# A linear attention block on one core: two row tiles transposed by DMA instead of TensorE, the fold's matmuls reordered, and the last row tile cut in four

## The chip, the cores and the metric

The kernel runs on one core of a Trainium2 chip. A core has a matrix engine (TensorE, PE in the profile, with PEld for its weight loads), a vector engine (DVE), a scalar engine (ACT), GpSimd (POOL) and a sync engine (SP), each with its own instruction queue, and sixteen DMA engines that SP's and ACT's queues feed here. Matmuls write to PSUM, eight banks of 512 float32 columns in 128 partitions; everything else lives in SBUF. The metric is the device time of one execution in microseconds (us), as the median of the runs.

## The reference

One batch of S = 2048 rows, D = 640 columns, 32 heads of 20 columns, all bfloat16.

```python
qkv = (x @ wqkv) split into q, k, v, each [32 heads, S, 20]
phi = lambda t: jnp.where(t > 0, t + 1, jnp.exp(t)) + 1e-6
pq, pk = phi(q), phi(k)
kv = jnp.einsum("bhsd,bhse->bhde", pk, v)
z = jnp.einsum("bhsd->bhd", pk)
num = jnp.einsum("bhqd,bhde->bhqe", pq, kv)
den = jnp.einsum("bhqd,bhd->bhq", pq, z)[..., None] + 1e-6
return (num / den, heads joined to [S, 640]) @ wo
```

## The kernel before, in words

The whole program is straight-line. A small planner (`Plan`) takes operations in the order in which the Python code adds them, puts each on the list of its engine, and works out from named reads and writes which semaphores it has to wait for. So each engine's order is the order of the calls, and where two calls are swapped, the work of every engine that they use is swapped. PSUM banks are named by hand.

**Load and k (0.8 to 27.8 us).** For k = x @ wk the matmul needs x with its columns on the partitions (`xT`). Row tiles have 128 rows. The first four, rows 0 to 511, are loaded as they are (`load_xn`, from SP's and ACT's queues, L230) and turned by TensorE against an identity (`transpose_x`, L194; DVE copies the result out of PSUM, L199). The constant NPE = 4 sets how many. All later rows come by the DMA's crossbar transpose, issued on SP's queue (`load_xT`, L184): first one load of 128 rows, then five of 256 and one of 128. The first of them waits until the last slice of wk has landed (L186). Behind them on SP's queue stand the loads of `load_rest`: wq, the plain x of row tiles 4 to 15 in three pieces, wv, wo. The k matmuls (`k_half`, L278) of row tiles 0 and 1 go column block by column block, in the order in which the slices of wk land, with the transposes of tiles 2 and 3 between; from tile 2 on a tile is ten matmuls of 320 columns, into two of eight banks, and ACT and DVE make phi of it (`k_phi`, L291 to L296).

**State by way of p (27.8 to 60.6 us).** Instead of v the kernel accumulates p = x^T phi(k) over all sixteen row tiles, one half of the columns at a time, five accumulators in banks 0 to 4 (`p_step`, L305), then copies the accumulators out, three by ACT and two by DVE (`p_out`, L317 and L320). DVE adds up z beside it. Between these matmuls stand single q tiles (`next_q` calls `q_tile`): five matmuls of 512 columns (L331), an exp on ACT (L339), two passes on DVE (L341, L344). There are twenty q tiles, four blocks of 512 rows by five column blocks; they use banks 5, 6 and 7 in turn (`take`).

**The fold (60.6 to 75.3 us).** When p is complete, the kernel (a) computes the eleventh q tile; (b) the normaliser of the first 1024 rows (`inverse`: sum matmuls L454, on ACT the logarithm L464 and exp L466, which gives a reciprocal) and spreads it over the partitions by DMA on SP's queue (`den_spread`, L471); (c) the state kv = wv^T p in 30 short matmuls (`kv_group`, L408) and cuts it to the heads' diagonal blocks on DVE (`kv_mask`, L425); (d) multiplies the state by wo in six pairs of matmuls (`w2_group`, L432), which ACT copies out (L436) and SP's queue lays out anew in `w2p` (`w2_rows`, L443). A q tile stands before each pair but the fifth, four more follow. In these q tiles' wake the five normalising multiplies of the first 512 rows run on DVE (`scale` fills a list, and each `next_q` takes one from it; `normalize`, L479).

**Output (75.3 us to the end).** A row tile of the output is pq @ w2p, two halves of five matmuls of 320 columns (`out_tile`, L487), copied out half by ACT (L509) and half by DVE (L512) and stored by SP's queue (L497). The normaliser of the second 1024 rows follows the second tile. The first tile needs the first 512 rows normalised and all of w2p. The last row tile (`out_last`) is cut in pieces of 320 and 160 columns (ACT) and 160 (DVE); SP stores the first 480 columns, ACT's queue the other 160.

Of the kernel before, what the change touches and what calls it, by code (L numbers as in the profile page):

```python
# [82 lines left out]
def bass_standalone__linear_attn_block__prompt_kernel(nc, x, wqkv, wo, out):  # L83
    B, S, D = x.shape
    assert (B, S, D) == (1, 2048, 640)
    H, DH = 32, 20
    NC_ = D // 128
# [7 lines left out]
    with contextlib.ExitStack() as ctx:  # L95
# [49 lines left out]
        def pool_const():  # L145
# [28 lines left out]

        NPE = 4
        XCH = [(128 * t, 128 * t + 128) for t in range(NPE + 1)] + [
            (a, min(a + 256, S)) for a in range(128 * NPE + 128, S, 256)]

# [3 lines left out]
        def load_xT():  # L182
            for i, (a, b) in enumerate(XCH[NPE:]):
                P.add("sp", lambda e, a=a, b=b: e.dma_start_transpose(  # L184
                    xT[:, :].rearrange("p (c s) -> p c s", s=S)[:, :, a:b], x[0, a:b, :]),
                    reads=[("wk", 4)] if i == 0 else [],  # L186
                    writes=[("xT", NPE + i)], dma=True)

# [36 lines left out]
        def load_wk():  # L225
            tl = mybir.InstLoadActFuncSet(
                name=nc.get_next_instruction_name(),
                act_func_set_id=ACT_TABLE_SET_LN_EXP, ins=[], outs=[])
            P.add("act", lambda e: e.add_instruction(tl), writes=["table"])
            for eng, what in (("sp", "x01 w01 w23 w45 x34"), ("act", "x12 w12 w34 x23")):  # L230
                for k in what.split():
                    a, b = int(k[1]), int(k[2])
                    if k[0] == "x":
                        load_xn(a, b, eng)
                    else:
                        P.add(eng, lambda e, a=a, b=b: e.dma_start(
                            wk[:, a * D:b * D].rearrange("p (c n) -> p c n", n=D),
                            wqkv[128 * a:128 * b, D:2 * D].rearrange("(c p) n -> p c n", p=128)),
                            writes=[("wk", c) for c in range(a, b)], dma=True)
# [4 lines left out]
        def load_rest():  # L244
            w_cols(wqn, 0, D, 0, "wqn", "sp")
            for a, b in ((4, 8), (8, 12), (12, 16)):
                load_xn(a, b, "sp")
# [76 lines left out]

        def q_tile(sbk, c, b):
            i = nq[0] % 3
            nq[0] += 1

            def mm(e):
                for d in range(NC_):  # L330
# [8 lines left out]
            P.add("act", lambda e: e.activation(t[:, :], bank(b), ACTF.Exp),  # L339
                  reads=[("bank", b), "table"], writes=[("eq", i)])  # L340
            P.add("dve", lambda e: e.tensor_scalar(  # L341
                t[:, :], t[:, :], 1.0, 1e-6, ALU.min, ALU.add),
# [85 lines left out]

        def w2_group(g, b):
            n = gsz[g]  # L430
            for h in range(2):
# [3 lines left out]
                    reads=[("kvt", g), "wog", "wog5"], writes=[("bank", b + h)])  # L435
            P.add("act", lambda e: e.copy(  # L436
                fold(w2g[0:n, g * D:(g + 1) * D]), two_banks(b, parts=n)),
                reads=[("bank", b), ("bank", b + 1)], writes=[("w2g", g)])

        def w2_rows(g):  # L440
# [54 lines left out]
        def out_dma(st, lo, hi, eng="sp"):  # L495
            j = st % 4
            P.add(eng, lambda e: e.dma_start(  # L497
                out[0, 128 * st:128 * st + 128, lo:hi], osb[j][:, lo:hi]),
                reads=[("osb", j, c) for c in range(lo // 160, hi // 160)],
                writes=[("out", st, lo)], dma=True)  # L500
            out_keys.append(("out", st, lo))
# [3 lines left out]
        def out_evac(st, b, lo, hi, eng):  # L505
            j = st % 4
            keys = [("osb", j, c) for c in range(lo // 160, hi // 160)]
            if eng == "act":
# [13 lines left out]
        def out_last(st, b):  # L522
            q = HALF // 2
            for n, (lo, hi, eng) in enumerate(((0, HALF, "act"), (HALF, HALF + q, "act"),
                                               (HALF + q, D, "dve"))):
                out_mm(st, b[n], lo, hi)
                out_evac(st, b[n], lo, hi, eng)
            out_dma(st, 0, HALF + q)
            out_dma(st, HALF + q, D, "act")

# [5 lines left out]
        warm(512, 512, 512, 512, 512, 512)  # L536
        order = "t0 t1 k00 k01 k10 k11 k02 k12 k03 k13 t2 k04 k14 t3"
        for k in order.split():
# [22 lines left out]

        def next_q(n=1):
            q_tile(*qs.pop(0), take())
            for _ in range(n):
# [24 lines left out]
        next_q()  # L589
        for st in range(NT):  # L590
            p_step(1, st)
# [37 lines left out]
        for st in range(4, NT - 1):  # L629
# [3 lines left out]
            out_tile(st, 2 * (st % 4) if st > 5 else 2 * (st % 2))  # L633
        out_last(NT - 1, (6, 7, 0))

# [36 lines left out]
```

## Time and profile before

| | us |
|---|---|
| median of 3 runs (101.2 to 102.3) | 101.67 |
| the profiled execution | 101.73 |
| its span, from first to last instruction | 100.0 |
| TensorE busy in it | 96.8 |
| DVE busy | 69.2 |
| ACT busy | 43.3 |

The profile is one execution on the hardware. Its page gives busy times by engine, a line of 40 equal slices of the span per engine (tenths of each slice), the chain of work that ended last, and groups of like instructions with their count, total and mean (ns) and, behind the bar, the idle time ahead of them. A timeline gives start, length, engine, line, operation, tiles and count; neighbours of one kind are merged, and PEld rows are left out where they only repeat PE. "SPq" and "ACTq" are queues that issue DMAs: their length is the issue, not the transfer; the time from issue to landing is a view of its own. Matmuls are pipelined: the time of one (0.3 us for 320 columns) is longer than the distance between two. Some matmul records can be missing, so that a count may be one short.

### The profile page before, as it was taken

The numbers are of one execution on the slowest core, as the hardware profiler recorded it, in microseconds if no ns is written. First come the engines' busy times: TensorE is split into PE (matmuls) and PEld (weight loads), VectorE is DVE, ScalarE is ACT, GpSimd is POOL, SyncE is SP. The second block draws the span as 40 slices with busy tenths as digits, with TensorE's granted clock in tenths as the row PEclk, the third lists the DMA queues.
The fourth block names the chain that finished last, engine by engine and source line by source line (L and its number), as shares of the span: only waits on it lengthen the run. The fifth ranks groups of instructions, "written<-read, shape, count | busy, mean of one in ns | idle before, by whom it ended". The sixth has DMA issues, their size and how long they took to land.

```text
span 100.0 us, 1793 instructions
## 1 busy us (share of the span) xinstructions
PE 96.8 (97%) x697; PEld 63.0 (63%) x703; DVE 69.2 (69%) x140; ACT 43.3 (43%) x76; POOL 3.3 (3%) x15
## 2 busy tenths in 40 slices
PE   6999999999999999999999999999999999999992
PEld 2556777777777565656667565756446677777771
DVE  0217988888889379799996445758899759853331
ACT  5005554445697220462132227398954523333322
POOL 6600000000000000000000000000000000000000
PEclk9999999999999999999999999999999999999999
DMA  2963999699999900000000000014440324523333
GB/s 56 308 226 71 185 205 137 132 236 377 371 365 289 191 14 0 0 3 0 7 0 0 0 0 0 25 34 123 120 136 1 117 70 153 213 95 120 131 131 131
DMA packets 17076, 11.93 MB, mean 119 GB/s; under 512 B 8749, under 2 KB 17069, under 8 KB 17069
## 3 DMA queue, kind: packets, MB, share of 16 engines
q1 hardware_dynamic: 16349, 11.14, 42.9%
q10 hardware_dynamic: 720, 0.70, 2.1%
q8 instruction: 5, 0.08, 0.3%
q14 instruction: 2, 0.02, 0.1%
HBM read 5.90 MB, written 2.62 MB: 85 GB/s over the span
## 4 chain that ended last, share of the span: by engine, by line
PE 91%; DVE 4%; ACT 2%; issue 1%
PE ps L278 22%; PE ps L487 22%; PE ps L305 22%; PE ps L331 16%; PE ps L269 3%; DVE pq L344 2%; PE ps L194 2%; PE ps L408 2%; PE ps L454 1%; ACT eq L339 1%; DVE pq L479 1%; PE ps L432 1%; DVE eq L341 1%; ACT w2g L436 1%; DVE osb L512 0%
## 5 line engine op out<-in xcount | busy, mean ns | idle before, releaser
L305 PE MATMUL ps<-pk,xn 128*128 128x320 bf16 x160 | 23.5, 299 | 0.0
L331 PE MATMUL ps<-xT,wqp 128*128 128x512 bf16 x94 | 23.1, 379 | 0.3
L278 PE MATMUL ps<-wk,xT 128*128 128x320 bf16 x160 | 22.8, 302 | 0.0
L487 PE MATMUL ps<-w2p,pq 128*128 128x320 bf16 (+1 forms) x165 | 22.1, 295 | 0.1
L339 ACT ACTIVATE eq<-ps 128x512 bf16<-128x512 f32 x20 | 12.0, 599 | 21.2 <-PE ps L331 20.7
L305 PEld LDWEIGHTS ps<-pk,xn 128*128 128x128 bf16 x160 | 15.6, 98 | 7.4 <-DVE pt L320 0.2
L487 PEld LDWEIGHTS ps<-w2p,pq 128*128 128x128 bf16 x165 | 15.8, 98 | 6.6 <-DVE pq L479 0.6
L278 PEld LDWEIGHTS ps<-wk,xT 128*128 128x128 bf16 x160 | 15.4, 99 | 6.6 <-DMA wk<-in_wqkv_dram 0.4
L291 ACT ACTIVATE ek<-ps 128x640 bf16<-128x640 f32 x16 | 11.2, 704 | 14.7 <-PE ps L278 14.7
L331 PEld LDWEIGHTS ps<-xT,wqp 128*128 128x128 bf16 x100 | 9.7, 97 | 9.0
L344 DVE SCALAR_TENSOR_TENSOR pq<-ps,eq 128x512 bf16<-128x512 f32 x20 | 13.8, 692 | 0.7
L296 DVE SCALAR_TENSOR_TENSOR pk<-ps,ek 128x640 bf16<-128x640 f32 x16 | 13.2, 825 | 0.5
L512 DVE CAST osb<-ps 128x320 bf16<-128x320 f32 (+1 forms) x16 | 7.7, 479 | 8.3 <-PE ps L487 8.2
L509 ACT CAST osb<-ps 128x320 bf16<-128x320 f32 (+1 forms) x17 | 7.0, 417 | 13.4 <-PE ps L487 12.1
L341 DVE TENSOR_SCALAR eq<-eq 128x512 bf16<-128x512 bf16 x20 | 5.8, 292 | 9.8 <-ACT eq L339 9.7
L479 DVE TENSOR_TENSOR pq<-pq,rd 128x512 bf16<-128x512 bf16 x20 | 7.7, 416 | 0.4 <-DMA rd<-rdc 0.4
L293 DVE TENSOR_SCALAR ek<-ek 128x640 bf16<-128x640 bf16 x16 | 5.2, 325 | 2.0 <-ACT ek L291 1.9
L199 DVE COPY xT<-ps 128x256 bf16<-128x256 bf16 (+1 forms) x8 | 2.2, 318 | 6.1 <-PE ps L194 6.1
L350 DVE TENSOR_TENSOR za<-pk 128x1280 f32<-128x1280 bf16 x4 | 5.8, 1481 | 0.0
L350 DVE TENSOR_TENSOR za<-za 128x1280 f32<-128x1280 f32 x3 | 4.4, 1480 | 0.0
L259 ACT COPY wqp<-wqn 128x640 bf16<-128x640 bf16 x5 | 4.3, 939 | 0.0
L436 ACT CAST w2g<-ps 120x640 bf16<-120x640 f32 (+1 forms) x6 | 4.0, 690 | 0.0
(38 smaller groups left out, 33.2 us busy)
## 6 DMA issues: line engine op xcount, KB each, us to landing
out_dram<-osb SPq DMA_DIRECT2D x15, 160.0 KB, 1.8
xn<-in_x_dram SPq DMA_DIRECT2D x3, 640.0 KB, 8.0
wqn<-in_wqkv_dram SPq DMA_DIRECT2D x1, 800.0 KB, 5.6
wv<-in_wqkv_dram SPq DMA_DIRECT2D x1, 800.0 KB, 11.2
wog<-in_wo_dram SPq DMA_DIRECT2D x1, 750.0 KB, 13.5
w2p<-w2g SPq DMA_DIRECT2D x5, 150.0 KB
rd<-rdc SPq DMA_DIRECT2D x8, 64.0 KB, 2.3
wk<-in_wqkv_dram SPq DMA_DIRECT2D x3, 160.0 KB, 4.4
```

Of the source, the lines that this page charges most:

```text
L278: r = e.matmul(bank(b + h, HALF), xT[:, c * S + 128 * st:c * S + 128 * st + 128], wk[:, c * D + HALF * h:c * D + HALF * (h + 1)], start=(c ...
L291: P.add("act", lambda e: e.activation(fold(t[:, :]), two_banks(b), ACTF.Exp), reads=banks + ["table"], writes=[("ek", st % 3)])
L296: P.add("dve", lambda e: e.scalar_tensor_tensor(fold(pk[:, st * D:(st + 1) * D]), two_banks(b), 0.0, fold(t[:, :]), ALU.max, ALU.add), rea ...
L305: r = e.matmul(bank(d, HALF), xn[:, st * D + 128 * d:st * D + 128 * d + 128], pk[:, st * D + HALF * h:st * D + HALF * (h + 1)], start=(st ...
L331: r = e.matmul(bank(b), wqp[:, d * D + 128 * c:d * D + 128 * c + 128], xT[:, d * S + BK * sbk:d * S + BK * (sbk + 1)], start=(d == 0), sto ...
L339: P.add("act", lambda e: e.activation(t[:, :], bank(b), ACTF.Exp), reads=[("bank", b), "table"], writes=[("eq", i)])
L344: P.add("dve", lambda e: e.scalar_tensor_tensor(pq[:, c * S + BK * sbk:c * S + BK * (sbk + 1)], bank(b), 0.0, t[:, :], ALU.max, ALU.add), ...
L350: P.add("dve", lambda e: e.tensor_tensor(d_ap, a, b, ALU.add), reads=ra + rb, writes=[dst])
L479: P.add("dve", lambda e: e.tensor_tensor(v, v, rd[i][:, BK * o:BK * (o + 1)], ALU.mult), reads=[("rd", i, 2 * o), ("rd", i, 2 * o + 1), (" ...
L487: r = e.matmul(bank(b, hi - lo), pq[:, c * S + 128 * st:c * S + 128 * st + 128], w2p[:, c * D + lo:c * D + hi], start=(c == 0), stop=(c == ...
L509: P.add("act", lambda e: e.copy(osb[j][:, lo:hi], bank(b, hi - lo)), reads=[("bank", b)], writes=keys)
L512: P.add("dve", lambda e: e.tensor_copy(osb[j][:, lo:hi], bank(b, hi - lo)), reads=[("bank", b)], writes=keys)
```

## The change

Three edits.

Crossbar: NPE goes from 4 to 2. Row tiles 2 and 3 get their transposed rows by two crossbar loads of 128 rows, ahead of six of 256; the first waits for the first slice of wk instead of the last. Their two transposes on TensorE go, and so do the early plain loads of x for tiles 2 and 3 on ACT's and SP's queues. That x is still needed for p: `load_rest` now loads tiles 2 to 15 in pieces of four, five and five.

Fold: the last two row tiles of p are accumulated in turn, bank by bank. The state matmuls and masks are added inside the eleventh q tile, between its exp and its DVE passes, and so stand ahead of the normaliser. DVE instead of ACT copies out the first pair, which stands right behind the normaliser's sum. Banks 4, 6, 7, 5 serve the q tiles after that. The multiplies of the first 512 rows are taken two behind the thirteenth q tile and one behind each of the next three; pairs three and four stand side by side; five q tiles follow the last pair instead of four. (`w2_rows` is called by `w2_group` itself.)

Last row tile: four pieces of 320 (ACT), 160 (DVE), 96 (ACT) and 64 columns (DVE) in four banks. The stores stay at 480 columns by SP and 160 by ACT's queue. The keys by which the planner follows the output are 32 columns wide instead of 160.

```diff
-        NPE = 4
-        XCH = [(128 * t, 128 * t + 128) for t in range(NPE + 1)] + [
-            (a, min(a + 256, S)) for a in range(128 * NPE + 128, S, 256)]
+        NPE = 2
+        XCH = [(128 * t, 128 * t + 128) for t in range(NPE + 2)] + [
+            (a, min(a + 256, S)) for a in range(128 * NPE + 256, S, 256)]
...
-                    reads=[("wk", 4)] if i == 0 else [],
+                    reads=[("wk", 0)] if i == 0 else [],
...
-            for eng, what in (("sp", "x01 w01 w23 w45 x34"), ("act", "x12 w12 w34 x23")):
+            for eng, what in (("sp", "x01 w01 w23 w45"), ("act", "x12 w12 w34")):
...
-            for a, b in ((4, 8), (8, 12), (12, 16)):
+            for a, b in ((2, 6), (6, 11), (11, 16)):
...
-        def q_tile(sbk, c, b):
+        def q_tile(sbk, c, b, between=None):
...
+            if between:
+                between()
             P.add("dve", lambda e: e.tensor_scalar(
...
-        def w2_group(g, b):
+        def w2_group(g, b, eng="act"):
...
-            P.add("act", lambda e: e.copy(
+            P.add(eng, lambda e: (e.copy if eng == "act" else e.tensor_copy)(
                 fold(w2g[0:n, g * D:(g + 1) * D]), two_banks(b, parts=n)),
                 reads=[("bank", b), ("bank", b + 1)], writes=[("w2g", g)])
+            w2_rows(g)
...
         def out_last(st, b):
-            q = HALF // 2
-            for n, (lo, hi, eng) in enumerate(((0, HALF, "act"), (HALF, HALF + q, "act"),
-                                               (HALF + q, D, "dve"))):
+            for n, (lo, hi, eng) in enumerate(((0, HALF, "act"), (HALF, 480, "dve"),
+                                               (480, 576, "act"), (576, D, "dve"))):
                 out_mm(st, b[n], lo, hi)
                 out_evac(st, b[n], lo, hi, eng)
-            out_dma(st, 0, HALF + q)
-            out_dma(st, HALF + q, D, "act")
+            out_dma(st, 0, 480)
+            out_dma(st, 480, D, "act")
...
-        order = "t0 t1 k00 k01 k10 k11 k02 k12 k03 k13 t2 k04 k14 t3"
+        order = "t0 t1 k00 k01 k10 k11 k02 k12 k03 k13 k04 k14"
...
-        for st in range(NT):
+        for st in range(NT - 2):
             p_step(1, st)
...
+        for d in range(NC_):
+            p_step(1, NT - 2, (d,))
+            p_step(1, NT - 1, (d,))
         p_out(1)
-        next_q()
+
+        def state_groups():
+            kv_group(0)
+            kv_mask(0)
+        next_q(between=state_groups)
         inverse(0)
         den_spread(0, (0, 1))
-        kv_group(0)
-        kv_mask(0)
-        small[:] = [5, 6, 7, 4]
-        for g in range(NG):
-            if g != 4:
-                next_q()
-            w2_group(g, 2 * ((g + 1) % 2))
-            w2_rows(g)
-            if g == 1:
-                scale(0, 0)
+        small.insert(0, 4)
+        w2_group(0, 2, "dve")
+        next_q()
+        w2_group(1, 0)
+        scale(0, 0)
+        next_q(2)
+        w2_group(2, 2)
+        w2_group(3, 0)
+        next_q()
+        w2_group(4, 2)
+        next_q()
+        w2_group(5, 0)
         den_spread(0, (2, 3))
-        for _ in range(4):
+        for _ in range(5):
             next_q()
...
-        out_last(NT - 1, (6, 7, 0))
+        out_last(NT - 1, (6, 7, 0, 1))
```

More of the change, by code (lines that the diff above doesn't have):

```diff
@@ L498, in out_dma @@
                 out[0, 128 * st:128 * st + 128, lo:hi], osb[j][:, lo:hi]),
-                reads=[("osb", j, c) for c in range(lo // 160, hi // 160)],
+                reads=[("osb", j, c) for c in range(lo // 32, hi // 32)],
                 writes=[("out", st, lo)], dma=True)
@@ L506, in out_evac @@
             j = st % 4
-            keys = [("osb", j, c) for c in range(lo // 160, hi // 160)]
+            keys = [("osb", j, c) for c in range(lo // 32, hi // 32)]
             if eng == "act":
@@ L560, in take, with next_q @@
             return small[-1]
-        def next_q(n=1):
-            q_tile(*qs.pop(0), take())
+        def next_q(n=1, between=None):
+            q_tile(*qs.pop(0), take(), between)
             for _ in range(n):
```

## The prediction

> **What bounds the kernel now.** I read the page first: the busy shares, the slices, the chain that ended last.
>
> ```profile
> span 100.0 us, 1793 instructions
> PE 96.8 (97%) x697; PEld 63.0 (63%) x703; DVE 69.2 (69%) x140; ACT 43.3 (43%) x76; POOL 3.3 (3%) x15
> PEclk9999999999999999999999999999999999999999
> GB/s 56 308 226 71 185 205 137 132 236 377 371 365 289 191 14 0 0 3 0 7 0 0 0 0 0 25 34 123 120 136 1 117 70 153 213 95 120 131 131 131
> PE 91%; DVE 4%; ACT 2%; issue 1%
> ...
> L331 PE MATMUL ps<-xT,wqp 128*128 128x512 bf16 x94 | 23.1, 379 | 0.3
> L278 PE MATMUL ps<-wk,xT 128*128 128x320 bf16 x160 | 22.8, 302 | 0.0
> ...
> rd<-rdc SPq DMA_DIRECT2D x8, 64.0 KB, 2.3
> ```
>
> TensorE is busy 97% of the span and carries 91% of the chain, at full granted clock in every slice. So an edit saves only what it takes off TensorE's list, what it closes of TensorE's few gaps, and what follows the last matmul. A busy share can hide matmuls that wait, so next I looked stage by stage, by windows (length; busy time of PE, PEld, DVE, ACT, POOL; clock; DMA).
>
> ```profile
> 27.80:60.60 32.80, 32.64 (x218) 20.79 (x220) 24.97 (x40) 11.88 (x20) 0.00 (x0) 1.00 0.24 63
> 60.60:75.30 14.70, 14.48 (x109) 8.06 (x110) 11.25 (x27) 10.74 (x21) 0.00 (x0) 1.00 0.27 75
> ```
>
> From 27.8 to 60.6 us no more than 0.16 us is open, and the change touches nothing there that TensorE waits for. In the fold (60.6 to 75.3) 0.22 us is open. That leaves three places: the first 12 us, the end of the fold, and the tail.
>
> **Part 1: rows 256 to 511 by the crossbar.** The timeline of the start (start, length, what):
>
> ```profile
> 4.72 2.73 PE L278 MATMUL ps<-wk,xT 128*128 128x320 bf16 x16
> ...
> 7.38 0.45 PE L194 MATMUL ps<-ident,xn 128*128 128x128 bf16 x5
> ...
> 7.67 0.71 PE L278 MATMUL ps<-wk,xT 128*128 128x320 bf16 x4
> ...
> 8.21 0.44 PE L194 MATMUL ps<-ident,xn 128*128 128x128 bf16 x5
> ...
> 8.49 7.78 PE L278 MATMUL ps<-wk,xT 128*128 128x320 bf16 x55
> ```
>
> A matmul of 320 columns is on record for 0.302 us (L278 above), so the last of a row starts 0.30 before the row's end, and the last row gives (7.78 - 0.30)/55 = 0.136 us a matmul and 1.36 us a row tile (ten of them). Before, row tile 2 starts at 8.49 and tile 4 at 8.49 + 2 x 1.36 = 11.21. The two L194 rows go away. The sixteen matmuls of the first row leave TensorE free at 4.72 + 2.73 - 0.30 + 0.14 = 7.29, four more follow (0.54), and tile 2 could start at 7.83: **0.66 us saved**. Four copies of DVE (L199) go too; they stood beside TensorE's matmuls, so they count nothing.
>
> Now tiles 2, 3 and then 4 must come by crossbar in time. The queue's waits, the issues on SP's queue, and the times from issue to landing:
>
> ```profile
> SPq L184 <- DMA wk<-in_wqkv_dram: 4.0, 1, 4.0
> ```
>
> ```profile
> 1.26 0.42 SPq L236 DMA_DIRECT2D wk<-in_wqkv_dram  x1
> ...
> 7.13 1.33 SPq L184 DMA_TRANSPOSE xT<-in_x_dram  x1
> ...
> 8.51 1.37 SPq L184 DMA_TRANSPOSE xT<-in_x_dram  x1
> ...
> 17.12 2.00 SPq L184 DMA_TRANSPOSE xT<-in_x_dram  x1
> ```
>
> ```profile
> wk<-in_wqkv_dram SPq DMA_DIRECT2D x1, 160.0 KB, 3.2
> ...
> xT<-in_x_dram SPq DMA_TRANSPOSE x1, 3.0
> ...
> xT<-in_x_dram SPq DMA_TRANSPOSE x1, 4.1
> ...
> xT<-in_x_dram SPq DMA_TRANSPOSE x1, 4.0
> ...
> DMA to landing us min/median/max: 3.0/4.4/6.1
> ```
>
> The four rows of landings belong to the four issues above them, in order; the last row is over all seven crossbar loads. Before, the first load (128 rows) waits for the last weights and goes out at 7.13; it lands at 10.1. The second (256 rows) goes out at 8.51 and lands at 12.6, the seventh lands at 21.1. The change lets the first go when the first weights land, 1.26 + 3.2 = 4.5. Call its loads X1 and X2 (128 rows each), then X3 to X8 (256 each). Issues follow each other at 1.38 us (7.13 to 8.51), whatever their rows:
> - X1 goes at 4.5, lands at 7.5, and tile 2 is due at 7.83: no wait.
> - X2 goes at 5.9, lands at 8.9, and tile 3 is due at 9.19: no wait.
> - X3 goes at 7.25. It is the first load of 256 rows behind one of 128, as the 8.51 row is, so 4.1 us: it lands at 11.35. Tile 4 is due at 7.83 + 2 x 1.36 = 10.55. **TensorE waits 0.80 us**, and tile 4 starts at 11.35 instead of 11.21.
>
> So the matmuls leave and a new wait takes their time: net +0.14. This wait has no row in the trace of before, so it has bounds. Below: with the shortest landing of any load, 3.0, X3 lands at 10.25 and there is no wait (0). Above: at the median, 4.4, the wait is 1.1; at the longest, 6.1, it is 2.8. I take 4.1, by the row of the same size and place. If X1 or X2 is late by some tenths, that costs nothing more, since X3 is what ends last.
>
> The loads behind X3: from 12.6 (row 896) to 21.1 (row 2048) the stream brought 256 rows in 1.9 us, and TensorE uses them in 2.72. No further wait. On SP's queue one plain load of x goes away ahead of the crossbar loads and one crossbar load is added; ACT's queue loses one load. At 1.9 us for 256 rows X8 lands at 11.35 + 5 x 1.9 = 20.9 against 21.1, so the loads queued behind it (wq, the rest of x in three uneven pieces, wv, wo) keep their times.
>
> Here the Trainium skill speaks against my wait. Its page "Advanced Engine Details and Errata", section "X-Bar Transpose (TRN2)", says that "TRN2 transpose DMAs are as fast as regular DMAs". The trace of before does not agree: the GB/s row has 205, 137 and 132 in the slices from 12.5 to 20.0 us, where crossbar loads run, and 377, 371 and 365 from 22.5 to 30.0, where plain loads do. By that rule X3 (0.33 MB) would need 0.9 us behind X2, an estimate at the plain loads' 371 GB/s, and TensorE would not wait: the sum would be -1.01 instead of -0.21.
>
> **Part 2: the fold.** Its timeline:
>
> ```profile
> 60.63 1.08 ACT L317 CAST pt<-ps 128x320 bf16<-128x320 f32 x3 [1.44 <-PE ps L305]
> ...
> 61.60 0.73 PE L454 MATMUL ps<-pq,zb 128*32 128x256 bf16 x20
> ...
> 62.27 1.61 PE L408 MATMUL ps<-pt,wv 128*128 128x120 bf16 x30
> ...
> 62.89 0.42 ACT L466 ACTIVATE rdc<-lb 128x256 bf16<-128x256 f32 x1
> 63.34 1.32 SPq L471 DMA_DIRECT2D rd<-rdc  x2
> 63.53 0.94 DVE L425 TENSOR_TENSOR kvt<-ps,bm 120x480 bf16<-120x480 f32 x3 [0.17 <-PE ps L408]
> ...
> 70.76 4.48 PE L331 MATMUL ps<-xT,wqp 128*128 128x512 bf16 x19
> ...
> 73.61 0.41 DVE L479 TENSOR_TENSOR pq<-pq,rd 128x512 bf16<-128x512 bf16 x1
> ...
> 74.87 0.41 DVE L479 TENSOR_TENSOR pq<-pq,rd 128x512 bf16<-128x512 bf16 x1
> ...
> 75.34 2.89 PE L487 MATMUL ps<-w2p,pq 128*128 128x320 bf16 x20
> ```
>
> TensorE's gap is at its end. The last q matmul starts at 70.76 + 4.48 - 0.38 = 74.86 (0.38 by L331's mean) and the next could start 0.22 later (nineteen starts in 4.10 us), at 75.08; the output matmuls start at 75.34, when the fifth normalising multiply (74.87 + 0.41) is done. **0.26 us** is lost. After the change the five multiplies stand behind q tiles 13 (two), 14, 15 and 16, and the last no longer behind tile 18. DVE's spacing there is 1.26 us a tile (73.61 to 74.87), so two tiles earlier is 2.5 us earlier: the wait goes.
>
> What comes late instead: the normaliser. The state matmuls (1.5 us) go ahead of its sum, so its reciprocal ends 1.5 later, at 64.8, and the first two spreads go out at 64.85 and 65.5. The page's median for such a spread is 2.3 us; with 3.0 they land by 68.5. Tile 13 leaves TensorE about 66.3 (63.6, then two pairs of 0.27 and two tiles of 1.08), so the first multiplies may wait up to 2 us on DVE, and the copies and q passes behind them with it. The fifth follows three tiles (3 x 1.26) after: 72.7 at the latest, against the 75.08 at which the output wants it.
>
> TensorE's own list in the fold is the same (ten q tiles, sum, state, six pairs). New waits on it: the state matmuls now start one q tile after the last accumulation (61.5) and need all five copies of the accumulated banks. In the order of before the last copy ends at 60.63 + 1.08 = 61.71; pairing the last two row tiles bank by bank frees the first bank 8 matmuls (1.1 us) before the last, so copies end near 61.1: no wait, and without that cover 0.2. The first pair of state-times-wo needs the masks: these start 1.26 behind the state matmuls (62.27 to 63.53) and take 0.94, so 62.8 to 63.7, while the pair is due behind state (1.45) and sum (0.66, from 61.60 to 62.27), at 63.6: 0 to 0.1. DVE takes one copy of 640 columns from ACT: between one and two of its copies of 320 columns (0.49, in the tail below), so up to 1.0 us, and it had 14.70 - 11.25 = 3.4 us free. Pairs 2 and 3 now stand side by side and need the banks of pairs 0 and 1 copied out; ACT had 4.0 us free, so I put that wait between 0 and 0.3, and take 0. With bank 4, long free, first in line, no q tile waits for a bank. I take -0.26, with 0 as the other end, since every margin is a few tenths and the gap to win is no larger.
>
> **Part 3: the last row tile.** The tail:
>
> ```profile
> 96.69 0.49 DVE L512 CAST osb<-ps 128x320 bf16<-128x320 f32 x1 [0.87 <-PE ps L487]
> 97.37 0.64 ACT L509 CAST osb<-ps 128x320 bf16<-128x320 f32 x2 [0.93 <-PE ps L487]
> 98.06 0.32 DVE L512 CAST osb<-ps 128x160 bf16<-128x160 f32 x1 [0.88 <-PE ps L487]
> 98.42 0.35 ACTq L497 DMA_DIRECT2D out_dram<-osb  x1
> ```
>
> ```profile
> 53.95 0.39 PE L390 MATMUL ps<-ones,zh 128*128 128x1 bf16 x10
> ```
>
> Matmul columns stay 640, in four pieces instead of three: five more matmuls, but of the same total length if short ones keep their pace. The last copy shrinks from 160 to 64 columns. Between 320 columns (0.49) and 160 (0.32) a column costs 1.06 ns of DVE, so 0.10 off; the ten short matmuls cost about 0.01 more. ACT's copy of 96 columns ends ahead of it, and the last transfer keeps its 40 KB. **-0.09**; at worst 0.
>
> The price of short matmuls is bounded by the last row: ten matmuls of one column, each with its own weights, lie within 0.39 us, so less than 0.043 apart. At the pace of 320 columns in 0.136, 96 columns take 0.041 and 64 take 0.027: held up by 5 x 0.016 = 0.08 at most, and I take 0. The Trainium skill, page "TensorE: Matmul & The Clock Gate", section "Wait — 56ns, not 53.3ns?", gives two floors, about 25 ns and, with hardware decode off, about 62 ns a matmul. By the second the pieces of 96 and 64 columns would cost 0.62 instead of 0.34 us, 0.28 more, an estimate from that page; the bound of 0.043 in this trace excludes it, so the sum goes without.
>
> **The sum.** The profiled execution took 101.73: a span of 100.0 and 1.73 around it; the median of the three runs is 101.67, so they are one case. -0.66 + 0.80 - 0.26 - 0.09 = **-0.21**, so 101.5.
>
> **Rivals.**
> - *Crossbar loads keep up* (14%). X3 lands by 10.8, next to nothing waits. For it: the first load took 3.0, not 4.1. Against: 10.1 to 12.6 is 2.5 us for the next 256 rows. -0.66 - 0.26 - 0.09 = -1.01: 100.7. It is also where the Trainium skill's rule above would lead.
> - *Weights hold the stream back: slower* (11%). Issued at 4.5, X1 stands in SP's queue behind weights that land until 7.1. If it moves only then, it lands 3.0 - 1.3 later at 8.8, X2 1.25 after, X3 2.5 after that, at 12.55: tile 4 is 1.34 late against 11.21, -0.35 for the rest, so 102.7. For it: 226 GB/s still moving in the slice from 5.0 to 7.5. Against: two loads of x are gone from these queues, and X1 needs only to land by about 7.8, not to be first. It decides from about 12.5 on.
> - *The fold gains nothing* (5%): a late spread or mask takes the 0.26 back: 101.8.
> - My forecast holds the other 70%, X3 between 10.8 and 12.3.
>
> **Chances.** About 1% is what a measurement can tell from no change, 1.02 us here. Faster takes half of the first rival and a little of the forecast: 0.11. Slower is the second rival: 0.12. The rest is within 1%: 0.77. Range: from the first rival's 100.7 to just short of the second's, 102.5.
>
> **What would show it.** Right: the first crossbar issue at 4.5; TensorE idle just under 1 us ahead of tile 4, ended by a crossbar load; output matmuls following the last q tile with no gap; a last copy of 64 columns near 0.22 us. Wrong: a wait ahead of tile 2 (second rival), none at all (first), or a q tile waiting for DVE.

## The result and the profile after

The changed kernel takes 101.56 us (median of 22 runs, 101.09 to 101.97) against 101.68 us for the kernel before (22 runs). The ratio is 0.9996, with a 95% interval of 0.9977 to 1.0016: no change that can be told, where 101.5 and "within 1%" were forecast. The profiled execution took 101.59 us. Its page:

```profile
span 100.1 us, 1780 instructions
...
PE 96.2 (96%) x692; PEld 62.7 (63%) x698; DVE 68.6 (68%) x138; ACT 43.0 (43%) x75; POOL 3.2 (3%) x15
...
PE 84%; DMA 8%; SPq 3%; DVE 2%; issue 1%; ACT 1%
...
L278 PE MATMUL ps<-wk,xT 128*128 128x320 bf16 x160 | 22.6, 301 | 0.7 <-DMA xT<-in_x_dram 0.7
```

TensorE has 0.6 us less work (96.8 before), but its share of the chain that ended last fell from 91% to 84%: DMA and SP's queue, which that row of the kernel before does not list, now hold 11%. The k matmuls (L278), which had no idle time ahead of them, have some, and a crossbar load ends it. The chain of waits of the changed kernel names the loads (start, length, what):

```profile
1.27 3.22 DMA wk<-in_wqkv_dram
4.51 1.33 SPq L184
5.88 1.26 SPq L184
7.18 4.54 DMA xT<-in_x_dram
...
11.77 16.47 PE ps L278 x120
```

Read it as a sentence: the first weights land at 4.49, SP issues two crossbar loads of 128 rows in a row, then X3, the first of 256 rows; that takes 4.54 us, and only then does TensorE go on, with row tile 4. From there TensorE is nearly all of the chain, as before. The same start in the timeline of TensorE's matmuls:

```profile
4.93 3.08 PE L278 MATMUL ps<-wk,xT 128*128 128x320 bf16 x20
8.45 3.05 PE L278 MATMUL ps<-wk,xT 128*128 128x320 bf16 x20 [0.43 <-DMA xT<-in_x_dram]
11.77 2.89 PE L278 MATMUL ps<-wk,xT 128*128 128x320 bf16 x20 [0.27 <-DMA xT<-in_x_dram]
```

The third row holds tiles 4 and 5 without a wait: (2.89 - 0.30) / 19 = 0.136 us a matmul. Tile 2 could start at 4.93 + 3.08 - 0.30 + 0.14 = 7.85 and starts at 8.45: a wait of 0.59 by the unrounded starts. The second row is longer than the third by a wait of 0.15 ahead of tile 3. Tile 4 could start at 8.45 + 3.05 - 0.30 + 0.14 = 11.34 and starts at 11.77: 0.43. (The figure in the bracket is only the part in which no matmul was in flight.) The issues' times to landing say which loads were late. X1's row:

```profile
xT<-in_x_dram SPq DMA_TRANSPOSE x1, 3.9
```

X1 landed at 8.40 instead of the 7.5 forecast, X2 (4.04 after its issue) at 9.92 instead of 8.9, X3 at 11.73 instead of 11.35.

In the fold, the timeline (starts of interest only):

```profile
61.94 1.60 PE L410 MATMUL ps<-pt,wv 128*128 128x120 bf16 x30
...
63.46 0.73 PE L457 MATMUL ps<-pq,zb 128*32 128x256 bf16 x20
...
69.34 0.76 DVE L482 TENSOR_TENSOR pq<-pq,rd 128x512 bf16<-128x512 bf16 x2 [0.61 <-DMA rd<-rdc]
...
70.14 5.56 PE L331 MATMUL ps<-xT,wqp 128*128 128x512 bf16 x24
...
73.47 0.41 DVE L482 TENSOR_TENSOR pq<-pq,rd 128x512 bf16<-128x512 bf16 x1
...
75.53 2.88 PE L490 MATMUL ps<-w2p,pq 128*128 128x320 bf16 x20
```

State (L410) now stands ahead of the sum (L457). The multiplies wait 0.61 us for their spread, as allowed for, and the fifth ends at 73.88. The last q matmul starts at 70.14 + 5.56 - 0.38 = 75.32 and the output 0.21 later, at the pace of the q matmuls: the gap is closed. From where the eleventh q tile can start (0.14 us behind the start of the last p matmul) to the first output matmul it is 14.67 us, 14.91 before.

The tail:

```profile
97.83 0.39 PE L490 MATMUL ps<-w2p,pq 128*128 128x96 bf16 x7
97.90 0.58 DVE L515 CAST osb<-ps 128x160 bf16<-128x160 f32 x2 [0.53 <-PE ps L490]
...
98.11 0.24 ACT L512 CAST osb<-ps 128x96 bf16<-128x96 f32 x1
98.25 0.33 SPq L500 DMA_DIRECT2D out_dram<-osb  x1
98.51 0.35 ACTq L500 DMA_DIRECT2D out_dram<-osb  x1
```

The second row merges DVE's two copies; the last one, of 64 columns, takes 0.22 us and ends at 98.48.

### The profile page after: what moved, and what is told of

It reads as the page before. It is cut to its first block, busy times and chain, and to the rows that moved or that the text cites. A ratio compares the mean times of both kernels' runs of the same rounds, so it can differ in the third digit from the quotient of the medians.

```text
span 100.1 us, 1780 instructions
## 1 busy us (share of the span) xinstructions
PE 96.2 (96%) x692; PEld 62.7 (63%) x698; DVE 68.6 (68%) x138; ACT 43.0 (43%) x75; POOL 3.2 (3%) x15
## 4 chain that ended last, share of the span: by engine, by line
PE 84%; DMA 8%; SPq 3%; DVE 2%; issue 1%; ACT 1%
PE ps L490 22%; PE ps L331 21%; PE ps L305 20%; PE ps L278 16%; DMA xT<-in_x_dram 5%; DMA wk<-in_wqkv_dram 3%; SPq L184 3%; PE ps L434 2%; PE ps L410 1%; PE ps L457 1%; DVE pq L346 1%; ACT eq L339 1%; DVE pt L320 0%; SPq L220 0%; DVE eq L343 0%
## 5 line engine op out<-in xcount | busy, mean ns | idle before, releaser
L278 PE MATMUL ps<-wk,xT 128*128 128x320 bf16 x160 | 22.6, 301 | 0.7 <-DMA xT<-in_x_dram 0.7
L490 PE MATMUL ps<-w2p,pq 128*128 128x320 bf16 (+3 forms) x170 | 22.1, 291 | 0.0
L278 PEld LDWEIGHTS ps<-wk,xT 128*128 128x128 bf16 x160 | 15.4, 98 | 7.8 <-DMA xT<-in_x_dram 1.7
L515 DVE CAST osb<-ps 128x320 bf16<-128x320 f32 (+2 forms) x17 | 7.9, 463 | 8.0 <-PE ps L490 6.8
L269 PE MATMUL ps<-const-bfloat16-1.0 128*128 128x512 bf16 x6 | 2.7, 623 | 0.8 <-PEq L668 0.8
L199 DVE COPY xT<-ps 128x256 bf16<-128x256 bf16 (+1 forms) x4 | 1.1, 320 | 3.5 <-PE ps L194 3.5
```

The lines of the kernel that those rows point to most:

```text
L278: r = e.matmul(bank(b + h, HALF), xT[:, c * S + 128 * st:c * S + 128 * st + 128], wk[:, c * D + HALF * h:c * D + HALF * (h + 1)], start=(c ...
L490: r = e.matmul(bank(b, hi - lo), pq[:, c * S + 128 * st:c * S + 128 * st + 128], w2p[:, c * D + lo:c * D + hi], start=(c == 0), stop=(c == ...
L515: P.add("dve", lambda e: e.tensor_copy(osb[j][:, lo:hi], bank(b, hi - lo)), reads=[("bank", b)], writes=keys)
```

## Experiments

**Theory A**, formed on this trace: a crossbar load that is issued while plain loads of weights are still coming in is late by about 1 us, and that delay, not the crossbar's own pace, is what makes tiles 2 and 3 wait. **Theory B**: the delay has nothing to do with the weights beside it, and stays when the load is kept apart from them. A third view is the prediction's second rival: the first load moves only when the last weights have landed. For the gap at the end of the fold the prediction named one holder, the fifth multiply; the rival, from that experiment on, is that the landing of w2p's last rows holds it too. For each kernel the numbers come from the profile; a ratio is against the kernel before on the same chip.

### The crossbar loads wait for the last weights again

```diff
-                    reads=[("wk", 0)] if i == 0 else [],
+                    reads=[("wk", 4)] if i == 0 else [],
```

> In the changed kernel the first crossbar load (X1, rows 256 to 383) took 3.9 us from issue (4.51) to landing (8.40); the first crossbar load of the kernel before took 3.0. Theory A: the weights still in flight stretch it. Theory B: a stream of crossbar loads close behind one another is that slow by itself. Here X1 goes out when the last weights have landed, about 6.6, with nothing plain in flight. A: X1 lands 3.0 after its issue, at 9.6, X3 4.1 after its own, at 13.5, and row tile 4 starts there, 1.7 us later than in the changed kernel (11.77); span near 101.8. B: X1 takes 3.9 again (10.5), X3 4.5 (13.9), tile 4 2.1 us later; span near 102.2.

It took 103.0 us in one run, with a span of 101.7. X1 goes out at 6.37, and its time to landing is

```profile
xT<-in_x_dram SPq DMA_TRANSPOSE x1, 2.8
```

1.06 less than in the changed kernel, for the same 128 rows in the same place of the queue. TensorE's matmuls:

```profile
4.76 3.10 PE L278 MATMUL ps<-wk,xT 128*128 128x320 bf16 x20
9.25 1.53 PE L278 MATMUL ps<-wk,xT 128*128 128x320 bf16 x10 [1.39 <-DMA xT<-in_x_dram]
11.37 1.53 PE L278 MATMUL ps<-wk,xT 128*128 128x320 bf16 x10 [0.58 <-DMA xT<-in_x_dram]
13.37 1.40 PE L278 MATMUL ps<-wk,xT 128*128 128x320 bf16 x9 [0.47 <-DMA xT<-in_x_dram]
```

Tile 4 starts at 13.37, 1.6 later than in the changed kernel, and the span is 1.6 longer. Issuing X1 1.86 earlier, as the change does, gains more than the delay costs. X2 took 3.57 instead of 4.04, and X3 4.27, hardly less than 4.54: Theory A explains X1, part of X2, and not X3. With the same trigger X1 goes out 0.76 earlier than in the kernel before (7.13): the last weights, without the early plain loads of x for tiles 2 and 3 beside them, were in at 6.35 instead of 7.12.

### The crossbar loads wait for nothing

```diff
-                    reads=[("wk", 0)] if i == 0 else [],
+                    reads=[],
```

> The crossbar loads wait for nothing and are issued right behind the weights on SP's queue, at about 2.7 instead of 4.51. Theory A (plain loads in flight stretch them, and they the plain loads): X1 takes more than 3.9, lands near 7.5, the weights that feed the last two steps of row tiles 0 and 1 land up to 0.5 later than 6.6, which costs nothing before 7.1; X3 (issued 5.4, 4.5 to 5 to land) lands at 9.9 to 10.4, ahead of 10.57, so the waits ahead of tiles 2, 3 and 4 (1.18 us together) go, and the kernel is about 1.1 us faster than the changed one: ratio to the kernel before 0.988 to 0.992. Theory B (the stream's own pace): X1 lands at 6.6, no waits, same time. A rival against both: the crossbar loads hold up the weights by more than 0.5 us, TensorE waits for weights instead, and the gain is half of that or less (0.995 and above).

100.77 us, ratio 0.9931 (0.9902 to 0.9961). X1 goes out at 2.67 and needs 4.60, the longest of all. No tile waits for the crossbar, but now a plain load is late: the second slice of wk, on ACT's queue,

```profile
wk<-in_wqkv_dram ACTq DMA_DIRECT2D x1, 160.0 KB, 4.3
```

against 3.4 in the changed kernel. In this kernel's waits:

```profile
PEld ps L278 <- DMA wk<-in_wqkv_dram: 0.7, 1, 0.7
```

TensorE stands 0.44 us longer ahead of the matmuls of that slice. In the twelve other profiles this slice lands at most 0.28 us behind the first one, here 1.13. So the delay seems to run both ways: plain loads hold up crossbar loads, and, by this one profile, crossbar loads plain ones. The gain came out somewhat below the forecast of 0.988 to 0.992. X1's 4.60 speaks for A.

### The crossbar loads wait for the first x

```diff
-                    reads=[("wk", 0)] if i == 0 else [],
+                    reads=[("xn", 0)] if i == 0 else [],
```

> The changed kernel with the first crossbar load waiting for the first rows of x (landed 3.5 to 3.8) instead of the first weights (4.5). X1 is issued at about 3.7, its transfer starts at 5.1, behind the landing of the second slice of wk (4.7) that was 0.9 us late when nothing was waited for. X3 is issued at 6.4 and lands 4.4 to 4.6 later, 10.8 to 11.0, tile 4 due at 10.57: 0.2 to 0.4 us of waits in all instead of 1.18. Ratio to the kernel before near 0.991, below the 0.9931 of the version without a wait. Rival: the transfers still hold up a slice of wk by 0.4 us or more; then TensorE's waits only move ahead of tile 2, and the ratio is 0.993 or above.

100.52 us, ratio **0.9878 (0.9839 to 0.9917)**, with the kernel of the last load experiment the fastest of all. X1 goes out at 3.59, 0.92 earlier than in the changed kernel, and the weights are not held up:

```profile
wk<-in_wqkv_dram ACTq DMA_DIRECT2D x1, 160.0 KB, 3.4
...
xT<-in_x_dram SPq DMA_TRANSPOSE x1, 3.8
```

(the second slice of wk; X1). TensorE:

```profile
4.81 5.82 PE L278 MATMUL ps<-wk,xT 128*128 128x320 bf16 x40
10.96 3.71 PE L278 MATMUL ps<-wk,xT 128*128 128x320 bf16 x26 [0.33 <-DMA xT<-in_x_dram]
```

Tiles 0 to 3 run through; only tile 4 waits, 4.81 + 5.82 - 0.30 + 0.14 = 10.47 to 10.96, 0.49 us. The first p matmul is at 27.27, against 28.08 in the changed kernel. X1 landed 0.66 after the last weights (6.70), and in the kernel before 2.97 after. So it does not stand still until they have landed: as a mechanism that rival is out.

### The old start with the new fold and tail

NPE, the trigger, the loads of x and the order of the k stage as in the kernel before; everything else as changed.

> Load stage of the kernel before, fold and last row tile of the changed kernel. If my account of the changed kernel is right (load stage +0.43 us, fold -0.23, last row tile -0.10), this takes 0.33 us off the kernel before: ratio 0.9967, span near 99.7, output matmuls starting 0.23 earlier than 75.34, at 75.10. Rival: the fold's gain is not there without the load stage's shift (a coincidence of DMA landings): ratio 0.999 to 1.000, output matmuls at 75.3.

101.29 us, ratio 0.9977 (0.9951 to 1.0004). The fold takes 14.67 us and the gap at its end is closed, as in the changed kernel: these parts do not need the new start. The forecast 0.9967 lies within the interval, and so does no change; the traces, not the times, carry this part. One of its waits is in the kernel before too, and in no kernel with the new start:

```profile
PEld ps L278 <- DVE xT L199: 0.3, 1, 0.3
```

The second half of row tile 2 waits for DVE's copy of tile 3's transpose out of a PSUM bank that it is to use. It makes the matmuls start 0.13 us later.

### The third crossbar load is 128 rows

```diff
-        XCH = [(128 * t, 128 * t + 128) for t in range(NPE + 2)] + [
-            (a, min(a + 256, S)) for a in range(128 * NPE + 256, S, 256)]
+        XCH = [(128 * t, 128 * t + 128) for t in range(NPE + 3)] + [
+            (a, min(a + 256, S)) for a in range(128 * NPE + 384, S, 256)]
```

> The changed kernel with the third crossbar load cut to 128 rows (512 to 639); the next are 256 rows again from 640. If the size of X3 sets the wait ahead of tile 4 (0.43 us in the changed kernel), X3 now lands about 1.3 us behind X2 (9.92), at 11.2, tile 4 is due at 11.33 and does not wait; tile 5 is due at 12.68 and its load lands near 13.0: the kernel is 0.1 to 0.4 us faster than the changed one. If it is the stream's pace in rows that holds TensorE, tile 5 waits for what tile 4 waited for before and the time is that of the changed kernel (within 0.1 us). The two waits ahead of tiles 2 and 3 (0.59 and 0.15) stay in both cases.

101.42 us, ratio 0.9991 (0.9967 to 1.0014). TensorE:

```profile
4.71 7.89 PE L278 MATMUL ps<-wk,xT 128*128 128x320 bf16 x50
12.87 1.80 PE L278 MATMUL ps<-wk,xT 128*128 128x320 bf16 x12 [0.27 <-DMA xT<-in_x_dram]
```

Tiles 2, 3 and 4 no longer wait, and tile 5 waits 0.44 (4.71 + 7.89 - 0.30 + 0.14 = 12.44 to 12.87), what tile 4 waited in the changed kernel. A smaller piece moves the wait one tile on; rows come no faster. In this run the last weights landed early, 1.56 us after X1's issue, and X1 took 2.72: what became of tiles 2 and 3 is Theory A again, and not the edit.

### The changed kernel once more

> The changed kernel once more, for the spread of its first crossbar load. Theory A (the tail of the weights, where it runs beside X1's transfer, stretches X1): X1 is issued about 4.5 and its transfer starts 1.4 later, at 5.9; if the last weights land by 6.3, X1 lands by 7.6 and tile 2 does not wait; if they land at 6.6, as in the first profile, X1 lands at 8.2 to 8.5 and tile 2 waits about 0.5. Theory B (no tie to the weights): X1 lands anywhere from 7.4 to 8.5 whatever the weights do. In both, tile 4 starts at X3's landing, 11.3 to 11.8.

101.25 us in one run. The last weights landed 0.21 earlier, at 6.39; X1 took 3.88, X3 4.24, and the first p matmul came at 27.68 instead of 28.08. With the other profiles this gives one table for Theory A: the last weights' landing after X1's issue, and what X1 took (128 rows in all of them).

| kernel | last weights after X1's issue, us | X1, issue to landing, us |
|---|---|---|
| before and four more that wait for the last weights | 0.0 | 2.75 to 2.95 |
| crossbar loads wait for the last weights again | 0.0 | 2.83 |
| third load 128 rows | 1.56 | 2.72 |
| last two p tiles in plain order (below) | 1.90 | 3.77 |
| changed, second run | 1.99 | 3.88 |
| changed | 2.09 | 3.89 |
| first x and 128 rows (below) | 2.94 | 3.62 |
| wait for the first x | 3.11 | 3.77 |
| wait for nothing | 3.97 | 4.60 |

Up to 1.6 us nothing is lost (the issue alone takes 1.33). From 1.9 on it is 0.7 to 1.9 us longer. The records of the DMA packets show what divides the two groups (crossbar loads move in packets of 256 bytes, these plain loads in packets of 1280). In the seven profiles in which X1 took under 3 us its first packet starts 0.26 us or more after the last packet of the plain loads has ended; in the six others it starts 0.08 to 0.92 us before that. Theory B, under which the column on the right would be level, is out. How a short overlap comes to cost about 1 us is not shown. X3's time does not follow this: 4.24 to 4.64 us in every kernel where it has 256 rows behind two of 128, with plain loads beside it or not.

### Both: waiting for the first x, and a third load of 128 rows

> The changed kernel with the first crossbar load waiting for the first rows of x (3.6) and the third load cut to 128 rows. With the first alone, one wait of 0.49 us was left, ahead of tile 4, for a third load of 256 rows that landed at 10.91 with tile 4 due at 10.47. The third load now lands about 1.3 behind the second (8.7), at 10.0 to 10.2, in time; the fourth (256 rows from 640) lands near 11.9 with tile 5 due at 11.83: waits of 0 to 0.2 in all. Another 0.3 us or so off: ratio to the kernel before 0.984 to 0.987, span near 99.0. Rival: one more issue on the queue costs the loads behind what tile 4 gains, tile 5 waits as long as tile 4 did, ratio 0.988 as without it.

100.52 us, ratio 0.9913 (0.9879 to 0.9947). No tile waits any more:

```profile
4.76 9.95 PE L278 MATMUL ps<-wk,xT 128*128 128x320 bf16 x69
```

The first p matmul is at 26.91, 0.36 earlier than with the first x alone. The forecast of 0.984 to 0.987 was missed: the interval ends at 0.9879. Against the first x alone the two were not on one chip; both medians are 100.52, and the ratios' intervals overlap, so the 0.36 us that the trace shows was not told apart in the time.

### The multiplies alone, in the kernel before

```diff
-                next_q()
+                next_q(2 if g == 2 else 1)
```

> The kernel before with one line changed: two normalising multiplies instead of one are taken behind the q tile of the third pair, so that the fifth stands behind q tile 17 instead of 18. The state matmuls stay behind the normaliser, the banks as they were. If the gap ahead of the output is that multiply alone, the output matmuls follow the last q matmul without a gap (0.22 us from start to start instead of 0.48) and this line is worth the fold's whole gain: span 0.25 less, ratio 0.9975. Rival: the gap is also held open by something that the rest of the fold's edit moves (the last rows of w2p, which land unseen); then 0.1 us or more of it stays.

102.01 us, ratio 1.0017 (0.9982 to 1.0052). The timeline around the output (line numbers are those of the kernel before, here and in the next two):

```profile
71.17 4.48 PE L331 MATMUL ps<-xT,wqp 128*128 128x512 bf16 x20
...
72.31 0.70 SPq L443 DMA_DIRECT2D w2p<-w2g  x1
...
74.01 0.41 DVE L479 TENSOR_TENSOR pq<-pq,rd 128x512 bf16<-128x512 bf16 x1
...
75.84 1.38 PE L487 MATMUL ps<-w2p,pq 128*128 128x320 bf16 x9 [0.19 <-issue]
```

The fifth multiply ends at 74.43, and TensorE, whose last q matmul starts at 71.17 + 4.48 - 0.38 = 75.27, waits all the same: 0.57 us from that start to 75.84. The last rows of w2p go out at 72.31, 3.5 before the output. In the kernel before they went out at 71.91 and the output started 3.4 later, within 0.1 of the multiply's end. The semaphore records have the landing of these rows: it is complete at 75.49, and TensorE's sequencer works off its waits for the six loads of w2p, two at a time, by 75.78. So the rival is right: w2p's rows hold the gap as well. In the kernel before those waits are worked off at 75.21 and the multiply ends at 75.28, so that without the multiply only 0.07 could be won there. Two readings are left: that the fifth multiply holds the output too, however early w2p is (Theory C), or that the gap goes once w2p is early enough (Theory D).

### The pairs early alone, and then both

In the kernel before, no q tile between pairs three and four, and five q tiles behind the last pair; in the second kernel two multiplies in the third round besides.

```diff
-            if g != 4:
-                next_q()
+            if g not in (3, 5):
+                next_q(2 if g == 2 else 1)
...
-        for _ in range(4):
+        for _ in range(5):
             next_q()
```

(The first kernel keeps `next_q()` in the second line.)

> The kernel before with the last pair of state-times-wo one q tile earlier: pairs three and four, and five and six, stand side by side, and five q tiles follow instead of four. The fifth normalising multiply stays behind q tile 18. In the run that only moved the multiplies, the fifth was done 1 us ahead of the end of the q tiles and the output still waited, 3.5 us behind the issue of the last rows of w2p. Theory C: in the kernel before both end at nearly the same time, the multiply at 75.28 and w2p near 75.3. Here the last rows go out about 1.1 us earlier; by C the multiply still holds the output: the gap from the last q matmul to the first output matmul stays at 0.45 to 0.48 us (0.22 is none). Theory D: w2p alone held it: the gap goes to 0.22.

102.79 us in one run. The last w2p rows go out 4.3 us ahead of the output, long enough, and the gap stays:

```profile
70.44 5.56 PE L331 MATMUL ps<-xT,wqp 128*128 128x512 bf16 x25
...
71.99 0.70 SPq L443 DMA_DIRECT2D w2p<-w2g  x1
...
75.81 0.41 DVE L479 TENSOR_TENSOR pq<-pq,rd 128x512 bf16<-128x512 bf16 x1
...
76.28 1.12 PE L487 MATMUL ps<-w2p,pq 128*128 128x320 bf16 x7 [0.28 <-DVE pq L479]
```

Here the fifth multiply ends at 76.22 and alone holds the output (w2p has landed at 75.19): 0.66 us from the last q start (75.62). Theory C gave 0.45 to 0.48; the multiply itself came 0.2 later against the q tiles than in the kernel before. Theory C, then, though not its size: two things held the same gap, and moving either one leaves it open.

> Both moves on the kernel before: the last pair one q tile earlier and two multiplies behind the q tile of the third pair. State matmuls still behind the normaliser. By theory C this is what closes the gap: the output follows the last q matmul after 0.22 us, and the fold (eleventh q tile to first output matmul) takes 14.67 us as in the changed kernel, against 14.91 before. Theory E: the state matmuls ahead of the normaliser are needed too; then 0.1 us or more of the gap stays.

102.06 us in one run; its weights landed latest of all, at 7.67, so the time is no verdict on the fold. Both together close the gap:

```profile
70.74 5.56 PE L331 MATMUL ps<-xT,wqp 128*128 128x512 bf16 x25
...
74.85 0.42 DVE L479 TENSOR_TENSOR pq<-pq,rd 128x512 bf16<-128x512 bf16 x1
...
76.14 1.25 PE L487 MATMUL ps<-w2p,pq 128*128 128x320 bf16 x8
```

The output follows the last q start (75.92) by 0.22. The fold takes 14.82 instead of the 14.67 expected. In the waits of this kernel stands the reason for the difference:

```profile
PEld ps L432 <- ACT w2g L436: 0.3, 1, 0.3
```

The sixth pair's weights wait for ACT's copy out of the bank. The fifth and sixth pair together take 0.72 us of TensorE where the third and fourth take 0.55: 0.17 of waiting. So two of the change's moves, the pairs together and the multiplies earlier, close the gap between them; the state matmuls ahead of the normaliser are not needed for that. What the rest of the new order is worth beyond it is the other 0.15 us; the changed kernel has a q tile between these two pairs.

### The last two p tiles in plain order, in the changed kernel

```diff
-        for d in range(NC_):
-            p_step(1, NT - 2, (d,))
-            p_step(1, NT - 1, (d,))
+        for st in (NT - 2, NT - 1):
+            p_step(1, st)
```

> The changed kernel with the last two row tiles of p in plain order again, tile by tile instead of bank by bank. If the pairing is the cover that I named, the last of the five copies of the accumulated banks now ends 0.2 us after the eleventh q tile leaves TensorE, and the state matmuls start 0.2 (0.1 to 0.3) us later than one q tile (1.08) after the last accumulation. Rival: ACT and DVE are ahead anyway, no wait, start 1.08 after as in the changed kernel.

101.85 us in one run. The timeline:

```profile
60.73 1.24 PE L331 MATMUL ps<-xT,wqp 128*128 128x512 bf16 x5
60.93 1.08 ACT L317 CAST pt<-ps 128x320 bf16<-128x320 f32 x3 [1.44 <-PE ps L305]
...
62.09 1.52 PEld L410 LDWEIGHTS ps<-pt,wv 128*128 128x128 bf16 x30 [0.61 <-DVE pt L320]
62.12 1.59 PE L410 MATMUL ps<-pt,wv 128*128 128x120 bf16 x30
```

The first state matmul now starts 0.31 us later behind the last p matmul than in the changed kernel, and waits for the last copy of p. The price put on the pairing's absence was 0.2 (0.1 to 0.3), so the cover is there and was worth a little more; the fold takes 14.97 us.

## Why the prediction came out right, and where its sum was off

The forecast, no change that can be measured, was right, and so was its reason: the transposes' time went into waits for the crossbar. In the two profiled executions, one of each kernel, the terms are these.

| term | forecast, us | measured, us |
|---|---|---|
| load and k stage (first p matmul, 27.66 to 28.08) | -0.66 + 0.80 = +0.14 | +0.43 |
| fold (eleventh q tile to first output matmul) | -0.26 | -0.23 |
| tail (first output matmul to the end) | -0.09 | -0.05 |
| sum, against the span's +0.1 | -0.21 | +0.15 |

**The load stage** is the mis-sized step in these two profiles. How far it was off in general they cannot say. The first p matmul came at 27.36 to 28.54 in the five profiles with the old start, 27.97 on average, and at 27.68 to 28.08 in three with the new one (the changed kernel twice, and with the last two p tiles in plain order), 27.91 on average. So +0.43 is not told apart from +0.14, nor from nothing; the medians of 22 runs lie 0.12 apart the other way. What the traces do show is which waits the stage consists of.

- "X1 goes at 4.5, lands at 7.5 ... no wait" and the same for X2 failed. The 3.0 came from a row in which the load waited for the last weights, and so ran without them; beside them it took 3.9. The two waits (0.59 and 0.15) cost nothing of their own, as the prediction said they would not: X3 is what ends last.
- X3's 4.1 was 4.5, and it went out 0.07 earlier: it landed 0.37 later than forecast, and tile 4 started 0.05 behind that. 4.1 was at the low edge; such loads took 4.0 to 4.6 in all profiles. This was inside the forecast's own range for X3 (10.8 to 12.3).
- "Tile 4 starts at 8.49 + 2 x 1.36 = 11.21" before was 0.14 too early. The row `8.49 7.78` has a wait of 0.13 inside it, which a mean over 55 starts spreads out. The waits of the kernel before name it (L278 behind DVE's copy L199); with the transposes it goes, a gain that was not counted.

So tile 4 started 0.42 later than forecast after the change (11.77 for 11.35) and 0.14 later than read off before it (11.35 for 11.21): +0.42 instead of +0.14, and that is carried unchanged to the first p matmul.

**Rivals.** The mark named for the second rival, a wait ahead of tile 2, was there, but not its price: tile 4 came at 11.77, not 12.55, and X1 moved before the last weights had landed (its first packet starts at 5.93, the weights were in at 6.60). The wait ahead of tile 4 was 0.43, not "just under 1 us": the two earlier waits had taken the rest of it, 1.18 in all. The first rival, by which crossbar loads keep up, is out for this place: X3's 256 rows (0.33 MB) came 1.8 us behind X2, at 180 GB/s, half of the plain loads' 377. "TRN2 transpose DMAs are as fast as regular DMAs", as the Trainium skill has it (page "Advanced Engine Details and Errata", section "X-Bar Transpose (TRN2)"), does not agree with that. Issued 0.9 us earlier, such a stream is nearly in time, and then the 1% that this rival promised is there (0.9878).

**The fold** gained what was forecast, -0.23 for -0.26. The spread was late by 0.61 on DVE where up to 2 was allowed, and no q tile waited for a bank. The state matmuls and the first pair together took 0.12 longer than at their own pace, and in the kernel before the sum had waited 0.09: so the whole gap of 0.26 was won, and 0.03 given back. But "until the fifth normalising multiply is done" was only half of the cause. The last rows of w2p held the same gap. The step failed without harm, since the change moves both, which was luck; as advice ("take the multiplies earlier") it would have gained nothing, as the run with the multiplies alone shows.

**The tail.** The last copy ends 0.10 earlier, 0.09 forecast (it takes 0.22 us for 64 columns). "The last transfer keeps its 40 KB" is true and not enough: its issue-to-landing time grew from 1.53 to 1.55 us in four profiles with the old tail to 1.58 to 1.60 in nine with the new one. SP's store of 480 columns now goes out 0.26 us ahead of it (98.25 and 98.51 above) instead of 0.38. That this is why was not tried. The short matmuls cost nothing, as taken: 96 columns start 0.042 apart and 64 columns 0.029, which the floor of 62 ns that the Trainium skill gives for hardware decode off (page "TensorE: Matmul & The Clock Gate", section "Wait — 56ns, not 53.3ns?") would not have let them, while its 25 ns floor does.

## What to carry to other kernels

A transfer's time to landing is that of its neighbours too: before moving a load ahead of the wait that kept it apart from others, look for a row in which it ran beside them, and if there is none, put the delay into the sum. Where a gap closes at two events within 0.1 us, read both as holders, and look for what else the waiting instruction reads. And a saving of engine time behind a stream of loads is worth only as much as the stream's first piece can be issued earlier: here the trigger alone decided between 0% and 1%.

## What the runs showed that was not expected

- A crossbar load of 128 rows took 2.7 to 2.95 us from issue to landing where the weights were in within 1.6 us of its issue, and 3.6 to 4.6 where they came in until 1.9 to 4.0 after it. In the other direction, beside an early crossbar load a plain load of 160 KB on the other queue took 4.3 instead of 3.4, in one profile.
- The five loads of weights were in between 6.24 and 6.70 us in the eight profiles with the new start, and between 6.45 and 7.67 in the five with the old one, where two more plain loads of x run behind and beside them. In those five, which are alike up to there, the first p matmul came anywhere from 27.36 to 28.54: a spread of 1.2 us, of the size of the spread of the kernel before over its runs (100.9 to 102.5).
- Load landings are only part of that spread. Of the first k matmuls none follow each other at 0.267 us in two of the five profiles, two in the kernel before, and six in the two others, instead of at 0.136; six cost 0.79 us. The clock row shows the full clock there (1.00), and no run tries the cause. With the new start such a slow beginning can vanish in the wait for the crossbar: the run with the third load of 128 rows has six too and still waits ahead of tile 5.
- A store of 40 KB landed 0.05 us later when another went out 0.26 instead of 0.38 us ahead of it, on another queue.
